# q times k as two 64-row by 120-column matmuls, scores packed without a gap, and one q tile loaded earlier

## The chip, the cores and the metric

The kernel runs on one core of one Trainium2 chip. The metric is the time of one execution in device microseconds, lower is better; the number quoted is the median of several runs. The profile is of one further execution.

## The reference, cut to what matters

Two parts follow each other: attention whose heads are mixed before and after the softmax ("talking heads"), then a bilinear feed-forward. Batch 4, 12 heads, 448 tokens, 64 channels a head; all in float32.

```python
scores = scale * np.matmul(q, k.transpose(0, 1, 3, 2))        # q times k
scores = np.einsum('bhij,hg->bgij', scores, w_pre)            # heads mixed
scores = scores - np.max(scores, axis=-1, keepdims=True)
attn = np.exp(scores)
attn = attn / (np.sum(attn, axis=-1, keepdims=True) + 1e-09)
attn = np.einsum('bhij,hg->bgij', attn, w_post)               # heads mixed again
x = np.matmul(attn, v)                                        # then [tokens, 768]
out = (x @ w_a * (x @ w_b)) @ w_out
```

## The kernel before

**Tiling of the attention.** Each batch's 448 query tokens are cut into chunks of 120, 120, 120 and 88. For each chunk, `qk(c, i)` makes the raw scores of two heads (i and i + 6) over all 448 keys. The channels of the two heads lie on SBUF rows 0 to 63 and 64 to 127, so `qk_head` is called with `g` = 0 and 1. For each head it issues two matmuls, one for each half of the chunk's tokens: a weight tile of 64 rows by 64 (or fewer) columns and a moving tile of 64 rows by 448. The first half goes to PSUM partitions 0 on, the second to partitions 64 on, so that for a chunk of 120 tokens the 4 partitions between hold nothing that is used. One `qk` is thus 4 matmuls, one in each quarter of the array; each float32 matmul stands in the trace as two records, each with a weight load of its own. One copy on VectorE or ScalarE (L304, L306) then moves both heads from PSUM (the one buffer of tag `t`) to the score tile `st[c]`.

**The order of tokens.** `spread_q` copies a loaded q tile (`qraw`, three heads of the chunk) into an order in which the five tokens of a half-block lie `nb` rows apart; `cut(n)` is where the second half begins (60 for n = 120).

**Units and steps.** A unit is 20 tokens of a chunk; there are 92 units, and the main loop runs one step `s` for each. `gather(u)` brings a unit's scores, by four SBUF-to-SBUF DMAs of 60 rows, into tiles `sb` in which heads and tokens share the partitions. `premix` (PSUM tile `mp`, L343) multiplies them with the mixing weights, `smax` takes maximum and exponential, `norm` prepares the second mixing matrix, `postmix` (`pp`, L389) applies it, `evac_p` copies it to `pt`, and `av` (`xp`, L427) multiplies with v. A step holds the premix of its unit, usually one `qk` for the next chunk, one `av` piece of the last group, and the postmix of the unit before. `premix`, `postmix` and `qk` are matmuls of 60 or 64 weight rows by 64 columns; `av` uses 128 rows by 64 columns; the matmuls of the feed-forward and of its first part (L637 to L639) 128 by 128.

**Start.** Before the loop, loads of q, k and the first 8 of 14 pieces of v (`V_EARLY`, L208 to L216) are issued on SyncE's queue (SP), in the order of the text. Up to unit 4, `gather` issues two of its four DMAs on SP and two on GpSimd's queue (POOL); later ones are all on POOL. POOL also runs `spread_q`. The `qraw` tiles have 3 buffers, so the fifth q tile waits for the copy of the second to be done.

**After step 90.** Feed-forward matmuls; the change does not touch them.

Of the kernel before, what the change touches and what calls it, by code (L numbers as in the profile page):

```python
# [22 lines left out]
def talking_heads_bilinear_kernel(  # L23
# [11 lines left out]
    nc = tc.nc  # L35
# [3 lines left out]
    QH = 5  # L39
    QB = 2 * QH  # L40
    QU = 2 * QB
    CHUNK = CHUNK_Q
    QG = 3
# [39 lines left out]
    chunks = []  # L83
    for b in range(B):
        t0 = 0
        while t0 < S:
            n = min(CHUNK, S - t0)
# [89 lines left out]
    def setup_w():  # L177
        nc.vector.memset(wp, 0.0)
        pre = wp[:, :QH * H].rearrange("p (i g) -> p i g", i=QH)
        shape = [64, QH, H]  # L180
        for e in range(2):
            rows = slice(64 * e, 64 * e + 64)
            nc.vector.tensor_tensor(
                pre[rows],
                wrep[rows, 0].unsqueeze(1).to_broadcast(shape),
                mask[rows, QH * e:QH * e + QH].unsqueeze(2).to_broadcast(shape),
                op=ALU.mult,
            )
        nc.vector.tensor_scalar(wp, wp, scale, None, op0=ALU.mult)
        nc.vector.tensor_tensor(tmask, mask[:, :QH], mask[:, QH:], op=ALU.add)  # L190
        shape = [128, H, QH]
        nc.vector.tensor_tensor(
            kf,
            wrep[:, 1].unsqueeze(2).to_broadcast(shape),
            tmask.unsqueeze(1).to_broadcast(shape),
            op=ALU.mult,
        )


    kt, kraw, qraw, qt = {}, {}, {}, {}  # L200
    st, sbt, mt, at, rss, krs, ptt, xps = {}, {}, {}, {}, {}, {}, {}, {}

    def load_v(b, i):
        g, i = divmod(i, V_PIECES // 2)
        to, of = vt[b % 2][g], v[b, g]
        if i < 3:
            heads = slice(2 * i, 2 * i + 2)
            nc.sync.dma_start(out=to[:C, heads], in_=of[:C, heads])  # L208
        elif i < 5:
            heads = slice(3 * (i - 3), 3 * (i - 3) + 3)  # L210
            nc.sync.dma_start(out=to[C:P, heads, :R - 1], in_=of[C:, heads, :R - 1])
        elif i == 5:
            for j in range(R - 1):
                nc.sync.dma_start(out=to[P:, :, j], in_=of[C + Y * j:C + Y * j + Y, :, R - 1])
        else:
            nc.sync.dma_start(out=to[C:, :, R - 1], in_=of[:C, :, R - 1])  # L216
# [4 lines left out]
    def part(half):  # L221
        return slice(0, 128) if half is None else slice(64 * half, 64 * half + 64)

    def load_k(b, i, half=None):
        if not half:
            if b == 0:
                if i == 0:
                    kraw["t"] = big.tile([128, G, S], F32, tag="pt", name="kraw")
                kraw[b, i] = kraw["t"][:, i]
            else:  # L230
                kraw[b, i] = k_p.tile([128, S], F32, tag="kraw", name="kraw", bufs=2)
        rows = part(half)
        nc.sync.dma_start(out=kraw[b, i][rows], in_=k[b, rows, i])

    def order_k(b, i, one=nc.vector.tensor_copy, two=nc.vector.tensor_copy):
        raw = kraw.pop((b, i)).rearrange("p (r x) -> p r x", r=R)
        kt[b, i] = k_p.tile([128, S], F32, tag="k", name="k")
        lo = kt[b, i][:, :R * C].rearrange("p (r x) -> p r x", r=R)
        hi = kt[b, i][:, R * C:].rearrange("p (r x) -> p r x", r=R - 1)
        one(lo, raw[:, :, :C])  # L240
        two(hi[:, :, :X], raw[:, :R - 1, C:])
        two(hi[:, :, X:], raw[:, R - 1, C:].rearrange("p (j l) -> p j l", j=R - 1))

    def load_q(c, j, half=None):
        b, t0, n = chunks[c]
        if not half:
            qraw[c, j] = q_p.tile([128, QG, CHUNK], F32, tag="qraw", name="qraw", bufs=3)[:, :, :n]
        rows, sl = part(half), slice(G * t0 + QG * j * n, G * t0 + QG * (j + 1) * n)
        nc.sync.dma_start(out=qraw[c, j][rows], in_=q[b, rows, sl].rearrange("d (h t) -> d h t", h=QG))

    def cut(n):
        nb, rest = divmod(n, QB)
        return QH * nb + min(rest, QH)

    def spread_q(c, j, eng=nc.gpsimd):
        n = chunks[c][2]
        nb = n // QB
        m, h0 = nb * QB, cut(n)
        t = q_p.tile([128, QG, CHUNK], F32, tag="q", name="q")[:, :, :n]
        raw = qraw.pop((c, j))  # L260
        for e in range(2):
            eng.tensor_copy(
                t[:, :, e * h0:e * h0 + QH * nb].rearrange("d h (i k) -> d h i k", k=nb),
                raw[:, :, :m].rearrange("d h (k i) -> d h i k", k=nb)[:, :, e * QH:(e + 1) * QH],
            )
        if m < n:
            r0 = h0 - QH * nb
            eng.tensor_copy(t[:, :, QH * nb:h0], raw[:, :, m:m + r0])
            if n - m > r0:
                eng.tensor_copy(t[:, :, h0 + QH * nb:], raw[:, :, m + r0:])  # L270
        qt[c, j] = t

    def qk_head(c, i, g, out):
        b, t0, n = chunks[c]
        rows = slice(D * g, D * g + D)
        h0 = cut(n)
        for e in range(2):
            cols = slice(0, 64) if e == 0 else slice(h0, n)
            nc.tensor.matmul(  # L279
                out[64 * e:64 * e + cols.stop - cols.start],  # L280
                lhsT=qt[c, i // QG][rows, i % QG, cols],
                rhs=kt[b, i][rows],
            )

    def qk(c, i, own=1):
        b, t0, n = chunks[c]
        m = 64 + n - cut(n)
        if c not in st:
            st[c] = (k_p if c % 3 == 2 else big).tile([128, H, S], F32, tag="s", name="s", bufs=1 if c % 3 == 2 else 2)
        if c <= 1 and i % 2 and i < QK_EARLY + 2 * (1 - c):  # L290
            for g in range(2):
                if i == 3:
                    sp = pp_t[g].rearrange("p x j t -> p (x j t)")[:, :S]
                else:
                    sp = ps.tile([128, 512], F32, tag="m", name="psq", bufs=3)[:, :S]
                qk_head(c, i, g, sp)
                nc.vector.tensor_copy(st[c][:m, g * G + i], sp[:m])
            return
        sp = ps.tile([128, 2, 512], F32, tag="t", name="pst", bufs=1)[:, :, :S]
        for g in range(2):  # L300
            qk_head(c, i, g, sp[:, g])
        to = st[c].rearrange("p (g i) s -> p i g s", g=2)[:m, i]
        if own:
            nc.vector.tensor_copy(to, sp[:m])  # L304
        else:
            nc.scalar.copy(to, sp[:m])  # L306

    def halves(n):
        return [(o, min(QH, n - o)) for o in range(0, n, QH)]

    def gather(u):
        c, o, n = units[u]
        sbt[u] = [sb_p.tile([128, S], F32, tag=f"sb{e}", name="sb") for e in range(2)]
        for i, (t, m) in enumerate(halves(n)):
            r = 64 * (i // 2)
            nb = chunks[c][2] // QB
            k_ = (o + t) // QB
            r0 = 64 * (t % QB // QH)
            if k_ < nb:
                rows = st[c][r0:r0 + QH * nb].rearrange("(i k) h s -> k i h s", k=nb)[k_]  # L320
            else:
                rows = st[c][r0 + QH * nb:r0 + QH * nb + m]
            (nc.sync if u <= AH and i % 2 else nc.gpsimd).dma_start(out=sbt[u][i % 2][r:r + m * H], in_=rows)  # L323
# [119 lines left out]
    for c in range(1, NC):  # L443
        b, t0, _ = chunks[c]
# [11 lines left out]
    for a in range(NA):  # L456
        b, u0, n = groups[a]
# [392 lines left out]
    with tc.manual_schedule():  # L850
# [16 lines left out]
        for i in range(G):  # L867
            if i == 1:
                spread_q(0, 1, nc.vector)
                setup_w()  # L870
            if i + 4 < G:
                load_k(0, i + 4)
                order_k(0, i + 4, pool, pool)
            if i == 2:
                load_q(1, 0)
                load_q(1, 1)
                for j in range(V_EARLY):
                    load_v(0, j)
            qk(0, i, 0)
# [2 lines left out]
        nxt_g = AH + 1  # L882
        for u in range(nxt_g):
            gather(u)
            if u == 2:
                load_q(2, 0)
                spread_q(2, 0)
            if u == 3:
                load_q(2, 1)
        for i in range(QK_EARLY):  # L890
            qk(1, i, 0)
        for r in range(2):
# [4 lines left out]
        for s in range(NU + 2):  # L897
# [3 lines left out]
            while nxt_g <= min(s + AH, NU - 1) and ready.get(units[nxt_g][0], -1) < s:  # L901
                gather(nxt_g)
                nxt_g += 1
# [110 lines left out]
        for n in range(NP * 2):  # L1014
            i, r = divmod(n, R6)
# [59 lines left out]
```

## Time and profile before

| | |
|---|---|
| three runs | 870.14, 873.02, 879.17 us; median 873.02 us |
| the profiled execution | 869.91 us, its span 868.2 us |
| PE busy | 839.9 us (97%) |
| PEld (weight loads) busy | 675.3 us (78%) |
| DVE, ACT, POOL busy | 500.0, 414.7, 476.3 us |
| L279 (q times k) | 728 records, 93.2 us busy |
| L343 (premix) | 720 records, 96.0 us busy |
| L389 (postmix) | 5040 records, 99.4 us busy |
| L427 (attention times v) | 1536 records, 93.3 us busy |

PE is the matmul part of TensorE, PEld its weight loads, DVE VectorE, ACT ScalarE, POOL GpSimd and SP SyncE. SPq is SP's queue of DMA issues. Matmul ends are modelled, so start times say more than durations: the difference between the starts of two groups of records is what the first group holds the engine for. Matmuls of different tiles of the array overlap, so busy times of two groups may overlap too.

### The profile page before, as it was taken

How to read it: one execution, taken by the hardware profiler on the slowest of the kernel's cores; microseconds unless marked ns; L12 is line 12 of the kernel's file. 1: busy time of each engine (PE TensorE's matmuls, PEld its weight loads, DVE VectorE, ACT ScalarE, POOL GpSimd, SP SyncE). 2: the span in 40 equal slices, each digit the busy share in tenths (PEclk: the TensorE clock that was granted, in tenths of full speed). 3: DMA queues.
4: the chain of work that ended last, by engine and by line, in shares of the span. 5: the costliest groups of instructions: out<-in, count | busy, mean ns of one | idle time of the engine just before them, and what ended most of it. 6: DMA issues, size and time to landing. Idle time of an engine off the chain costs nothing.

```text
span 868.2 us, 26219 instructions
## 1 busy us (share of the span) xinstructions
PE 839.9 (97%) x10612; PEld 675.3 (78%) x10612; DVE 500.0 (58%) x989; ACT 414.7 (48%) x864; POOL 476.3 (55%) x591
## 2 busy tenths in 40 slices
PE   8899999999999899999999999999999999999998
PEld 4455665656556565798999999999999998999997
DVE  5577677868787777355533433354445345655762
ACT  3576676767767688544323322332233145333330
POOL 5775686767757876026447433668666743222220
PEclk9999999999999999999999999999999999999999
DMA  7797799788867986673644643656665497564551
GB/s 188 183 194 174 164 219 192 180 183 200 203 161 180 209 218 137 182 242 134 199 133 162 191 152 132 217 192 237 221 233 183 146 327 291 199 232 182 203 204 66
DMA packets 105730, 165.90 MB, mean 191 GB/s; under 512 B 50278, under 2 KB 81618, under 8 KB 105610
## 3 DMA queue, kind: packets, MB, share of 16 engines
q1 hardware_dynamic: 77482, 126.54, 46.6%
q0 software_dynamic: 28128, 37.68, 19.2%
q8 instruction: 84, 1.38, 0.7%
q14 instruction: 36, 0.29, 0.1%
HBM read 84.16 MB, written 41.29 MB: 144 GB/s over the span
## 4 chain that ended last, share of the span: by engine, by line
PE 78%; DMA 9%; POOL 4%; issue 3%; DVE 3%; SPq 1%; ACT 1%; DVEq 0%; POOLq 0%
PE xp L427 6%; PE pp L389 6%; PE pb L639 6%; PE pa L637 6%; PE pa L638 6%; PE pa L639 6%; PE pb L638 6%; PE pb L637 6%; PE po L757 6%; PE po L758 6%; PE pst L279 6%; PE po L756 6%; PE mp L343 5%; DMA sb<-s 4%; POOL sb L323 3%
## 5 line engine op out<-in xcount | busy, mean ns | idle before, releaser
L323 POOL DMA_DIRECT2D sb<-s x350 | 201.9, 591 | 55.5 <-PE mp L343 19.5
L356 ACT ACTIVATE a<-mp,nm 124x448 f32<-124x448 f32 x180 | 112.7, 631 | 63.2 <-DVE nm L353 63.2
L353 DVE TENSOR_REDUCE nm<-mp 124x1 f32<-124x448 f32 x180 | 104.0, 618 | 55.1 <-PE mp L343 54.3
L659 DVE TENSOR_TENSOR hf<-pb,sa 128x448 f32<-128x448 f32 x47 | 29.3, 624 | 169.2 <-PE pb L639 153.7
L427 PEld LDWEIGHTS xp<-pt,v 128*64 128x64 f32 x1536 | 73.8, 136 | 61.9 <-issue 43.5
L643 ACT COPY sa<-pa 128x448 f32<-128x448 f32 x47 | 25.2, 536 | 174.6 <-PE pa L639 174.6
L406 ACT COPY pt<-pp 128x480 f32<-128x480 f32 x176 | 91.2, 575 | 33.9 <-PE pp L389 33.4
L389 PE MATMUL pp<-kr,a 60*64 60x60 f32 x5040 | 99.4, 222 | 7.6 <-issue 7.1
L389 PEld LDWEIGHTS pp<-kr,a 60*64 60x64 f32 x5040 | 86.6, 135 | 24.9 <-issue 13.7
L639 PE MATMUL pb<-xhl,wl 128*128 128x448 f32 x282 | 102.3, 363 | 0.9 <-POOL wl L622 0.9
L637 PE MATMUL pb<-xhl,wh 128*128 128x448 f32 x282 | 102.2, 362 | 0.0
L638 PE MATMUL pb<-xhl,wh 128*128 128x448 f32 x282 | 102.2, 362 | 0.0
L279 PE MATMUL pst<-k,q 64*64 64x448 f32 (+1 forms) x728 | 93.2, 549 | 8.0 <-DVE s L304 4.8
L343 PE MATMUL mp<-sb,wp 60*64 60x448 f32 x720 | 96.0, 550 | 3.6 <-DMA sb<-s 3.0
L637 PE MATMUL pa<-xhl,wh 128*128 128x448 f32 x264 | 95.7, 362 | 0.0
L638 PE MATMUL pa<-xhl,wh 128*128 128x448 f32 x264 | 95.7, 362 | 0.0
L639 PE MATMUL pa<-xhl,wl 128*128 128x448 f32 x264 | 95.7, 362 | 0.0
L427 PE MATMUL xp<-pt,v 128*64 128x120 f32 (+1 forms) x1536 | 93.3, 265 | 0.8 <-ACT pt L406 0.8
L628 POOL TENSOR_TENSOR wl<-v,wh 128x768 fp32r<-128x768 f32 x21 | 39.2, 1867 | 98.9 <-ACT wh L627 96.4
L757 PE MATMUL po<-hhl,wh 128*128 128x448 f32 x252 | 91.6, 363 | 1.6 <-DVE hhl L715 1.6
L758 PE MATMUL po<-hhl,wl 128*128 128x448 f32 x252 | 91.4, 363 | 0.0
L756 PE MATMUL po<-hhl,wh 128*128 128x448 f32 x252 | 91.3, 362 | 0.0
(117 smaller groups left out, 1432.3 us busy)
## 6 DMA issues: line engine op xcount, KB each, us to landing
sb<-s POOLq DMA_DIRECT2D x346, 105.0 KB, 5.2
hhl<-hd SPq DMA_DIRECT2D x42, 448.0 KB
v<-in_w_ab_dram SPq DMA_DIRECT2D x22, 768.0 KB
hd<-hf SPq DMA_DIRECT2D x48, 224.0 KB
v<-in_w_out_dram SPq DMA_DIRECT2D x12, 768.0 KB
wod<-cw SPq DMA_DIRECT2D x21, 384.0 KB
v<-wod SPq DMA_DIRECT2D x21, 384.0 KB
xhl<-xd SPq DMA_DIRECT2D x24, 224.0 KB
```

Of the source, the lines that this page charges most:

```text
L279: nc.tensor.matmul(out[64 * e:64 * e + cols.stop - cols.start], lhsT=qt[c, i // QG][rows, i % QG, cols], rhs=kt[b, i][rows],)
L323: (nc.sync if u <= AH and i % 2 else nc.gpsimd).dma_start(out=sbt[u][i % 2][r:r + m * H], in_=rows)
L343: nc.tensor.matmul(mt[u, i // 2][col:col + M], lhsT=wp[r:r + m, :M], rhs=tiles[i % 2][r:r + m])
L356: nc.scalar.activation(a[:m], mp[:m], ACTF.Exp, bias=nm[:m], scale=1.0, accum_out=rss[u][:m, j:j + 1])
L389: nc.tensor.matmul(pp_t[i][C * e:C * e + C, H * r:H * r + H, j, :m], lhsT=at[u, j][rows, x:x + C], rhs=kr[rows, j, :, :m],)
L427: nc.tensor.matmul(xp[64 * e:64 * e + 64, p % 3, :n], lhsT=vt[b % 2][g][:, h % G, r], rhs=ptt[a][:, r, h, :n], start=(r == 0), stop=(r == ...
L637: nc.tensor.matmul(o, lhsT=hh[:, off + k], rhs=x[:, 0, k], start=first, stop=False)
L638: nc.tensor.matmul(o, lhsT=hh[:, off + k], rhs=x[:, 1, k], start=False, stop=False)
L639: nc.tensor.matmul(o, lhsT=ll[:, off + k], rhs=x[:, 0, k], start=False, stop=last)
L756: nc.tensor.matmul(po, lhsT=hh[:, k], rhs=t[:, 0, k], start=(k == 0), stop=False)
L757: nc.tensor.matmul(po, lhsT=hh[:, k], rhs=t[:, 1, k], start=False, stop=False)
L758: nc.tensor.matmul(po, lhsT=ll[:, k], rhs=t[:, 0, k], start=False, stop=(k == KH2 - 1))
```

## The change

`qk_head` issues one matmul for each head, with a weight tile of 64 rows by all n tokens of the chunk (120 or 88 columns), which writes PSUM partitions 0 to n - 1. The score rows have no gap any more: copies move n rows (`m`) and `gather` finds the second half at row `cut(n)`. In the start, the load of the third chunk's first q tile, `load_q(2, 0)`, stands ahead of the early loads of v, where it stood behind the gathers of units 0 to 2, and its `spread_q` stands behind all five first gathers, where it stood behind the third.

```diff
     def qk_head(c, i, g, out):
         b, t0, n = chunks[c]
         rows = slice(D * g, D * g + D)
-        h0 = cut(n)
-        for e in range(2):
-            cols = slice(0, 64) if e == 0 else slice(h0, n)
-            nc.tensor.matmul(
-                out[64 * e:64 * e + cols.stop - cols.start],
-                lhsT=qt[c, i // QG][rows, i % QG, cols],
-                rhs=kt[b, i][rows],
-            )
+        nc.tensor.matmul(out[:n], lhsT=qt[c, i // QG][rows, i % QG], rhs=kt[b, i][rows])
 
     def qk(c, i, own=1):
         b, t0, n = chunks[c]
-        m = 64 + n - cut(n)
+        m = n
...
-            r0 = 64 * (t % QB // QH)
+            r0 = cut(chunks[c][2]) * (t % QB // QH)
...
             if i == 2:
                 load_q(1, 0)
                 load_q(1, 1)
+                load_q(2, 0)
                 for j in range(V_EARLY):
                     load_v(0, j)
             qk(0, i, 0)
...
         for u in range(nxt_g):
             gather(u)
-            if u == 2:
-                load_q(2, 0)
-                spread_q(2, 0)
             if u == 3:
                 load_q(2, 1)
+        spread_q(2, 0)
         for i in range(QK_EARLY):
             qk(1, i, 0)
```

## Rows read from the trace of the kernel before

**Rows 1.** Page, chain that ended last: share of the span by engine.
```profile
PE 78%; DMA 9%; POOL 4%; issue 3%; DVE 3%; SPq 1%; ACT 1%; DVEq 0%; POOLq 0%
```

**Rows 2.** Windows: stretch, its length, busy us (records) by engine, PEclk, DMA share, GB/s.
```profile
53.00:77.00 24.00, 21.68 (x528) 12.59 (x520) 17.41 (x49) 15.45 (x39) 15.77 (x28) 1.00 0.93 194
...
77.00:230.00 153.00, 148.57 (x3724) 92.45 (x3723) 112.67 (x278) 109.55 (x269) 108.37 (x203) 1.00 0.83 188
230.00:262.00 32.00, 29.24 (x737) 17.03 (x733) 27.08 (x72) 22.17 (x55) 17.86 (x32) 1.00 0.77 173
262.00:292.00 30.00, 30.00 (x742) 18.31 (x732) 22.01 (x54) 22.06 (x54) 24.81 (x44) 1.00 0.83 194
...
304.00:327.00 23.00, 23.00 (x560) 14.02 (x552) 17.93 (x42) 19.23 (x46) 16.85 (x31) 1.00 0.90 217
```

**Rows 3.** Windows of line 279 (q times k) alone: PE and PEld busy (records).
```profile
77.00:230.00 153.00, 42.60 (x344) 14.04 (x344) 1.00 0.83 188
230.00:262.00 32.00, 7.70 (x64) 1.95 (x64) 1.00 0.77 173
262.00:292.00 30.00, 9.21 (x72) 2.88 (x72) 1.00 0.83 194
...
304.00:327.00 23.00, 6.62 (x56) 2.10 (x56) 1.00 0.90 217
```

**Rows 4.** Timeline of PE, one step from 151.55 us: start, length, line, tiles, records.
```profile
151.55 0.94 PE L343 MATMUL mp<-sb,wp 60*64 60x448 f32 x8
152.31 0.93 PE L279 MATMUL pst<-k,q 64*64 64x448 f32 x8
153.17 1.04 PE L427 MATMUL xp<-pt,v 128*64 128x120 f32 x16
154.15 1.04 PE L389 MATMUL pp<-kr,a 60*64 60x60 f32 x56
155.01 0.56 PE L343 MATMUL mp<-sb,wp 60*64 60x448 f32 x4
```

**Rows 5.** Timeline of PE: from 128 weight columns to 64, rows unchanged.
```profile
366.86 0.37 PE L638 MATMUL pst<-xhl,wh 128*128 128x448 f32 x1
367.06 0.36 PE L639 MATMUL pst<-xhl,wl 128*128 128x448 f32 x1
367.35 0.75 PE L427 MATMUL xp<-pt,v 128*64 128x88 f32 x14
```

**Rows 6.** Timeline of PE: the first 128-column matmuls behind postmix.
```profile
348.34 0.47 PE L637 MATMUL pst<-xhl,wa 128*128 128x448 f32 x1
348.65 0.37 PE L638 MATMUL pst<-xhl,wa 128*128 128x448 f32 x1
```

**Rows 7.** Timeline of SP's queue in the start: DMA issues by line.
```profile
6.19 2.22 SPq L208 DMA_DIRECT2D v<-in_v_dram  x3
...
12.86 0.62 SPq L208 DMA_DIRECT2D v<-in_v_dram  x1
14.58 6.76 SPq L323 DMA_DIRECT2D sb<-s  x6
21.39 1.03 SPq L249 DMA_DIRECT2D qraw<-in_q_dram  x1
```

**Rows 8.** Timeline of DVE: the copy of the second q tile.
```profile
8.99 0.72 DVE L262 COPY q<-qraw 128x180 f32<-128x180 f32 x2
```

**Rows 9.** Timeline of POOL: third chunk's q tile, then gathers of units 3 on.
```profile
26.11 0.93 POOL L262 COPY q<-qraw 128x180 f32<-128x180 f32 x2 [7.42 <-DMA qraw<-in_q_dram]
26.98 4.59 POOL L323 DMA_DIRECT2D sb<-s  x8
```

**Rows 10.** Timeline of PE: premix of unit 0 and of unit 3, idle before.
```profile
18.86 1.55 PE L343 MATMUL mp<-sb,wp 60*64 60x448 f32 x5 [0.79 <-DMA sb<-s]
...
31.14 1.52 PE L343 MATMUL mp<-sb,wp 60*64 60x448 f32 x5 [2.25 <-DMA sb<-s]
```

**Rows 11.** Windows: the granted clock behind that wait (seventh figure).
```profile
32.00:34.00 2.00, 2.00 (x19) 1.49 (x14) 0.57 (x2) 0.00 (x0) 1.47 (x3) 0.50 0.87 191
```

## The prediction

> **What bounds the kernel now.** I read the chain that ended last first. By engine it is 78% TensorE [rows 1], so an edit on PE counts, if it falls in a stretch where PE sets the pace. The change touches only the attention, and so the windows over that part come next. Between 77 and 230 us PE is busy 148.6 of 153 us, between 262 and 292 and between 304 and 327 us without a gap [rows 2]. Between 230 and 262 us it idles 2.8 us, and in 53 to 77 us 2.3 us with the DMA engines 93% busy [rows 2]: there something else decides now and then. Then the timeline of one step shows what a step consists of: premix, q times k, attention times v, postmix, and after 3.46 us (155.01 - 151.55) the next premix, with nothing idle between [rows 4]. In such steps a longer q times k lengthens the step by as much. The number of them: the records of line 279 are 8 to a `qk`, so 344, 72 and 56 records are 43, 9 and 7 steps [rows 3], together 59; another 8 lie between 230 and 262 us.
>
> The second thing to read is the start. Premix of unit 3 waits 2.25 us for its gather [rows 10]; that gather was issued on POOL at 26.98 us, behind a copy which had waited 7.42 us for the third chunk's q tile [rows 9]; and that tile was issued on SP only at 21.39 us, behind six gathers [rows 7]. Behind the gap the granted clock is at 0.50, that is at 1.2 instead of 2.4 GHz, for a whole window of 2 us [rows 11].
>
> **The body of q times k.** Now four matmuls of 64 by 64 fill the four quarters of the array; afterwards two of 64 by 120 fill its two halves. Premix, four quarters too, holds the engine 0.76 us (152.31 - 151.55) for two passes [rows 4], so one pass of 448 columns takes 0.38 us with all quarters at work. Two halves that work at once need the same two passes: 0.76 us. Halving the number of matmuls and weight loads thus saves nothing here, since the passes set the time. Copies of 120 instead of 124 rows take as long, because they go by columns. The gathers read as many rows as before. Both at nothing.
>
> **What the wider weights cost.** From premix to q times k nothing about the tile changes today, and the 0.76 us are bare. From q times k to attention times v (64 by 64 to 128 by 64) it is 0.86 us for the same two passes (153.17 - 152.31) [rows 4]: 0.10 us are lost at the change of tile. Is it the rows or the columns that cost? One place in the trace changes columns alone: from 128 by 128 to 128 by 64 it takes 0.29 us where the steady spacing is 0.20 us (367.35 - 367.06 against 367.06 - 366.86) [rows 5], so 0.09 us are lost with the rows unchanged. After the change premix (64 by 64) to q times k (64 by 120) is such a change of columns, in every step, and q times k to attention times v remains one: one more per step, 0.10 us. The Trainium skill (TensorEngine Tiling (Array Packing), Key Properties) says that changing the tiling mode, not just the tile, drains the TensorE; the trace agrees, with the 0.09 and 0.10 us just read, and by that rule the change costs time.
>
> The second cost lies behind such a change. The first 128-column matmul behind postmix holds the engine 0.31 us (348.65 - 348.34) [rows 6] against 0.20 us steady [rows 5]: its weights are not there yet, 0.11 us. For 120 columns I take 120/128 of it, 0.10 us, once, as the loads of the two row halves can run side by side. Sum for each `qk`: 0.10 + 0.10 = 0.20 us. Bounds: 0.09 us if the weights still come ahead of time, 0.31 us if two loads follow each other (0.10 + 2 x 0.105).
>
> Over the 59 steps: 59 x 0.20 = 11.8 us. The others I cost at nothing: between 230 and 262 us and before 77 us, waits for loads and copies cover 0.2 us a step (PE idles 2.8 us in some nine steps, 2.3 us in some six) [rows 2]; without that cover it is 14 x 0.2 = 2.8 us more. In the first steps a `qk` is followed by a copy out of its single PSUM buffer, and PE waits for it.
>
> **The moved load.** `load_q(2, 0)` takes the buffer of the second q tile, whose copy on DVE is done at 8.99 + 0.72 = 9.71 us [rows 8]. SP reaches the load before 6.19 us, where v starts today [rows 7], and stands there until 9.71 us. Queued behind it are the eight pieces of v (10 DMAs), and behind these SP's half of the gathers. With 0.6 us for the load itself, as a piece of v takes [rows 7], v starts at about 10.3 us, 4.1 us late, and ends at 13.48 + 4.1 = 17.6 us; the gathers of units 0 to 2, which start at 14.58 us today [rows 7], start at 17.6 us. So units 0 to 2 are 3.0 us late, and PE's 0.79 us before premix 0 [rows 10] becomes 3.8 us.
>
> On the other side POOL no longer waits: its gathers of units 3 and 4 go out at 26.11 - 7.42 = 18.69 us, eight microseconds earlier [rows 9]. Unit 3 now waits for SP's half: 17.6 + 6.76 us for the six before it = 24.4 us, 2.25 us for its own two (a third of 6.76) [rows 7], then 2.0 us to land (premix 0 starts at 18.86 us [rows 10], and the first two of the six are out at 14.58 + 2.25 = 16.8 us): about 28.6 us instead of 31.14 us, a gain of 2.5 us. The slow clock I leave out of the sum: the long gap before premix 0 is likely to bring it there instead. Bounds: a loss of 3 us if the delay of units 0 to 2 is never made up; a gain of 5.5 us if v costs SP nothing, so that its two gathers of unit 3 follow the six as early as the q load does today (21.39 + 2.25 + 2.0 = 25.6 us). What follows up to 77 us runs with DMA engines 93% busy [rows 2]; as all of it is paced by the steps, I let the gain through.
>
> **Sum.** 11.8 - 2.5 = 9.3 us. On the profiled execution, 869.9 us with its span of 868.2, that gives 879.2 us; it lies 3.1 us below the median of the runs, so that on the median, 873.0 us, the forecast is **882 us**, about 1.1% slower.
>
> **Rivals.** (a) The weights still arrive during premix, and only the change of tile costs: 59 x 0.10 - 2.5 = 3.4 us, 876 us. For it: weight loads do run ahead within one tile shape. Against: the 0.31 us [rows 6].
> (b) Width alone costs nothing in this place, since both row halves stay: then only the start is left, -2.5 us, 870.5 us, at best 867.5 us: not slower. It decides if premix to q times k stays at 0.76 us. Against: the 0.29 us with unchanged rows [rows 5].
> (c) The gap in SP's queue is not made up by unit 3, and the start loses its 3 us: 873 + 11.8 + 3 = 888 us. For it: v ends 4 us later in my own sum.
> (d) Two tiles of 64 rows by 128 columns do not run at once: 0.76 us more in each of the 59 + 8 `qk`, 51 us, with the rest 933 us or more. Against: premix does run both row halves at once [rows 4]; but in 64-column tiles, and no row shows 64 by 128.
>
> **How the numbers follow.** Forecast 0.45; (a) 0.17; (b) 0.13; (c) 0.18; (d) 0.07. A measurement of this kernel tells about 1%, 8.7 us, from no change. The forecast's own range is 877 to 889 us: 0.15 to 0.25 us a step with a start between -5 and 0 us. The whole range, 869 to 893 us, takes in (a), (c), most of (b), and leaves (d) out; its upper end is 59 steps at 0.31 us, 18.3 us, with a start at +1.7. Slower by over 1% (above 881.7 us): about 0.6 of the forecast, most of (c), all of (d), 0.51. Within 1%: the rest of the forecast, (a) and most of (b), 0.42. Faster by over 1% (below 864.3 us) needs more than (b)'s best start: 0.07.
>
> **What would show it.** A step between 77 and 230 us should last 3.66 us instead of 3.46; premix to q times k 0.86 instead of 0.76 us, q times k to attention times v 0.96 instead of 0.86 us. If the former stays at 0.76 us, (b) holds; if the latter stays at 0.86, (a); if it is above 1.5 us, (d). In the start, v should begin near 10 us on SP, POOL's 7.4 us wait be gone, premix 0 come near 22 us and premix of unit 3 near 28.6 us; if the latter comes behind 31 us, (c) holds. The feed-forward behind 370 us should take as long as before; if it does not, something is at work that I have not seen.

## The result, and the profile after

The changed kernel is slower by 0.6%: 878.22 us median against 872.28 us, ratio 1.0057 with a 95% interval of 1.0036 to 1.0079, or 5.0 us (3.1 to 6.9). The forecast was 882 us with a range of 869 to 893. The profiled execution has a span of 878.8 us, against 868.2: these two executions lie 10.6 us apart, twice the measured difference, so what is read from them stage by stage adds up to too much.

Line numbers are 7 lower from `qk_head` on: L276 is the q-times-k matmul (before L279), L336 premix, L382 postmix, L420 attention times v, L316 the gathers, L346 the maximum.

The page's chain that ended last, by engine, has TensorE at 86% now, where it had 78% [rows 1]:

```profile
PE 86%; DMA 3%; DVE 3%; POOL 2%; issue 2%; SPq 1%; ACT 1%; DVEq 0%; POOLq 0%
```

The timeline of PE over one step of a 120-token chunk (start, length, line, tiles, records), to be held against [rows 4]:

```profile
92.93 0.94 PE L336 MATMUL mp<-sb,wp 60*64 60x448 f32 x8
93.80 1.02 PE L276 MATMUL pst<-k,q 64*120 64x448 f32 x4
94.74 1.04 PE L420 MATMUL xp<-pt,v 128*64 128x120 f32 x16
95.71 1.04 PE L382 MATMUL pp<-kr,a 60*64 60x60 f32 x56
96.57 0.94 PE L336 MATMUL mp<-sb,wp 60*64 60x448 f32 x8
```

Premix to q times k takes 0.87 us (it was 0.76), q times k to attention times v 0.94 us (0.86), the step 3.64 us (3.46). That is 0.11 us at the change of tile and 0.08 us for weights that are not there yet, 0.19 us together. The timeline of PEld shows the latter: in the kernel before, weight loads of q times k begin 0.37 us ahead of its first matmul at 152.31 us [rows 4], in the changed kernel with it, at 93.79 us (first before, then after):

```profile
151.94 0.15 PEld L279 LDWEIGHTS pst<-k,q 64*64 64x64 f32 x4 [0.22 <-issue]
...
93.79 0.29 PEld L276 LDWEIGHTS pst<-k,q 64*120 64x120 f32 x4 [0.70 <-ACT pt L399]
```

For a chunk of 88 tokens the second figure shrinks with the columns:

```profile
152.81 0.94 PE L336 MATMUL mp<-sb,wp 60*64 60x448 f32 x8
153.68 0.99 PE L276 MATMUL pst<-k,q 64*88 64x448 f32 x4
154.59 1.04 PE L420 MATMUL xp<-pt,v 128*64 128x120 f32 x16
```

Here q times k holds the engine 0.91 us instead of 0.94. The two row halves do run at once: four records in the time of eight.

The start looks quite unlike what was forecast. SP's queue, as in [rows 7]:

```profile
4.57 5.79 SPq L249 DMA_DIRECT2D qraw<-in_q_dram  x3
10.41 1.83 SPq L208 DMA_DIRECT2D v<-in_v_dram  x3
...
16.03 1.61 SPq L208 DMA_DIRECT2D v<-in_v_dram  x1
17.76 11.48 SPq L316 DMA_DIRECT2D sb<-s  x8
```

The third of the three q loads waits for its buffer; v begins at 10.41 us instead of 6.19, and the gathers at 17.76 instead of 14.58. Then eight gathers take 11.48 us to go out, 1.4 us each; before, six took 6.76 us. POOL, as in [rows 9]:

```profile
15.49 5.77 POOL L316 DMA_DIRECT2D sb<-s  x10 [2.65 <-DVE s L290]
21.17 1.02 POOL L262 COPY q<-qraw 128x180 f32<-128x180 f32 x2
```

POOL does not wait for the q tile any more, and its ten gathers of units 0 to 4 go out in one run. But the first unit's data from SP's queue take 7.38 us to land, by the chain of waits,

```profile
17.76 7.38 DMA sb<-s
```

and PE, whose premix of unit 0 stands in [rows 10] at 18.86 us, does half of it at 19.50 us and the other half at 25.18 us:

```profile
19.50 1.45 PE L336 MATMUL mp<-sb,wp 60*64 60x448 f32 x4 [1.24 <-DMA sb<-s]
25.18 2.89 PE L336 MATMUL mp<-sb,wp 60*64 60x448 f32 x4 [4.23 <-DMA sb<-s]
```

In this gap the granted clock falls, and it is 0.50 from 24 to 32 us (windows; the seventh figure is the clock), where [rows 11] have that for one window of 2 us:

```profile
24.00:28.00 4.00, 2.82 (x5) 0.57 (x5) 0.62 (x1) 0.37 (x1) 0.00 (x0) 0.50 0.49 140
28.00:32.00 4.00, 4.00 (x15) 1.25 (x16) 2.59 (x6) 1.08 (x4) 1.73 (x3) 0.50 0.59 177
```

How far the units have come is read from the start of their first maximum on DVE, which follows premix. Against the kernel before, the changed one is 6.3 us late at unit 0, 8.8 at unit 2, 4.2 at unit 4, 2.1 at unit 13 and 9.0 at the last unit; behind the attention another 1.6 us come in these two executions. In them the start thus lost 2 us where it was to gain 2.5, and the steps from 13 on lost 7 where they were to lose 12.

The 1.6 us stand in the feed-forward, which was to take as long as before, and the granted clock shows them. Both kernels have a wait of PE for DVE of 1.28 us there; behind it the clock falls in the changed kernel (first line) and not in the kernel before (second line):

```profile
730.00:733.00 3.00, 3.00 (x11) 2.66 (x11) 1.16 (x2) 1.19 (x4) 0.00 (x0) 0.61 1.03 415
...
721.00:724.00 3.00, 3.00 (x16) 2.81 (x16) 1.16 (x2) 1.21 (x4) 0.00 (x0) 1.00 1.02 415
```

The experiment with the load behind v, further below, has the same fall behind the same wait (its clock is 0.50 from 727 to 729 us), the other experiments that move the start do not: it is not tied to the wide weights, and from one profile of each kernel no run tells how often it comes.

### The profile page after: what moved, and what is told of

Read it like the earlier page. It is cut to its first block, busy times and chain, and to the rows that moved or that the text cites. A ratio compares the mean times of both kernels' runs of the same rounds, so it can differ in the third digit from the quotient of the medians.

```text
span 878.8 us, 25451 instructions
## 1 busy us (share of the span) xinstructions
PE 854.2 (97%) x10228; PEld 671.6 (76%) x10228; DVE 501.9 (57%) x989; ACT 415.2 (47%) x864; POOL 476.2 (54%) x591
## 3 DMA queue, kind: packets, MB, share of 16 engines
q0 software_dynamic: 28128, 37.68, 17.6%
## 4 chain that ended last, share of the span: by engine, by line
PE 86%; DMA 3%; DVE 3%; POOL 2%; issue 2%; SPq 1%; ACT 1%; DVEq 0%; POOLq 0%
PE xp L420 9%; PE pp L382 8%; PE pst L276 8%; PE mp L336 7%; PE pb L632 6%; PE pa L630 6%; PE pa L631 6%; PE pa L632 6%; PE pb L631 6%; PE pb L630 6%; PE po L750 6%; PE po L751 6%; PE po L749 6%; POOL sb L316 1%; DMA sb<-s 1%
## 5 line engine op out<-in xcount | busy, mean ns | idle before, releaser
L316 POOL DMA_DIRECT2D sb<-s x350 | 201.6, 589 | 68.3 <-PE mp L336 36.2
L346 DVE TENSOR_REDUCE nm<-mp 124x1 f32<-124x448 f32 x180 | 104.1, 619 | 66.5 <-PE mp L336 66.1
L420 PEld LDWEIGHTS xp<-pt,v 128*64 128x64 f32 x1536 | 73.9, 136 | 58.8 <-issue 38.1
L382 PE MATMUL pp<-kr,a 60*64 60x60 f32 x5040 | 97.8, 222 | 6.3 <-issue 5.7
L382 PEld LDWEIGHTS pp<-kr,a 60*64 60x64 f32 x5040 | 84.4, 134 | 24.7 <-issue 16.9
L336 PE MATMUL mp<-sb,wp 60*64 60x448 f32 x720 | 93.9, 549 | 5.6 <-DMA sb<-s 5.5
L276 PE MATMUL pst<-k,q 64*120 64x448 f32 (+1 forms) x364 | 93.2, 588 | 3.4 <-DVE s L297 1.9
L420 PE MATMUL xp<-pt,v 128*64 128x120 f32 (+1 forms) x1536 | 93.4, 265 | 1.1 <-ACT pt L399 0.8
```

The lines of the kernel that those rows point to most:

```text
L276: nc.tensor.matmul(out[:n], lhsT=qt[c, i // QG][rows, i % QG], rhs=kt[b, i][rows])
L336: nc.tensor.matmul(mt[u, i // 2][col:col + M], lhsT=wp[r:r + m, :M], rhs=tiles[i % 2][r:r + m])
L382: nc.tensor.matmul(pp_t[i][C * e:C * e + C, H * r:H * r + H, j, :m], lhsT=at[u, j][rows, x:x + C], rhs=kr[rows, j, :, :m],)
L420: nc.tensor.matmul(xp[64 * e:64 * e + 64, p % 3, :n], lhsT=vt[b % 2][g][:, h % G, r], rhs=ptt[a][:, r, h, :n], start=(r == 0), stop=(r == ...
```

## The experiments

Each runs against the kernel before. Its ratio carries a 95% interval; 0.1% is 0.87 us.

### The unchanged kernel, timed like an experiment

> The kernel before, unchanged, timed like an experiment: how far apart two programs that are the same come out. Theory: ratio 1.000, within 0.3%. Rival (the comparison puts every experiment some 0.3% above, as the four runs that moved loads, copies or gathers, 1.0026 to 1.0039, make one suspect): 1.003.

Measured: 0.9985 (0.9955 to 1.0015). In this series nothing is added by the comparison itself, and differences below 0.3% are not told from nothing. In its profile units 1 and 2 come 1.0 and 1.2 us later than in the first profile of the same kernel, and unit 13 comes 1.1 us earlier; shifts of that size between two profiles say nothing.

### Only the wide weights

The hunks of `qk_head`, `qk` and `gather`'s row are kept, the moved load and copy are put back.

> Only the wide weights of the change; loads and copies of the start stand as in the kernel before. Theory (tile price): the two traces show premix to q times k at 0.868 us instead of 0.757 and q times k to attention times v at 0.946 instead of 0.863, 0.19 us for each qk; from step 13 to the end of the attention the changed kernel fell 7.0 us further behind (2.06 us to 9.03 us). With the start untouched this kernel should be slower than the one before by about 5 to 8 us, ratio 1.006 to 1.009, and unit 3's premix should come at the 31 us of before. Rival (the start is the whole loss): within 2 us of the kernel before.

Measured: 1.0043 (1.0013 to 1.0073), 3.7 us (1.1 to 6.3). The wide weights alone make the kernel slower; its steps show the same 0.87 and 0.94 us. Of the rival (within 2 us) only the lower end of the interval is left, 1.1 to 2 us. The size is below what was expected, and unit 3's maximum came 2.0 us later than before in this profile, unit 13's 2.4 us, not at the same time: the changed kernel's 2 us at unit 13 need not be all due to the moved load.

### Only the moved load and copy

Column halves stay.

```diff
                 load_q(1, 1)
+                load_q(2, 0)
                 for j in range(V_EARLY):
...
-            if u == 2:
-                load_q(2, 0)
-                spread_q(2, 0)
...
+        spread_q(2, 0)
```

> Only the moved load and copy; q times k in column halves as before. Theory (start loses): SP waits with the load for the second q tile's copy, v and the first gathers come late, and unit 2's maximum should come 7 to 9 us later than the 26.0 us of before; the transfers behind it are paced by the steps and find freer DMA engines, so that at 77 us 0 to 3 us are left: ratio 1.000 to 1.004. Rival (the start gains, as predicted): 2.5 us faster, ratio 0.997.

Measured: 1.0032 (0.9996 to 1.0067). The maxima of units 0 to 4 come at 27.21, 31.00, 33.66, 37.28 and 41.32 us, where the kernel before has 20.72, 23.38, 26.04, 33.43 and 37.95 us:

```profile
27.21 1.32 DVE L353 TENSOR_REDUCE nm<-mp 124x1 f32<-124x448 f32 x2 [8.61 <-PE mp L343]
31.00 1.15 DVE L353 TENSOR_REDUCE nm<-mp 124x1 f32<-124x448 f32 x2
33.66 1.15 DVE L353 TENSOR_REDUCE nm<-mp 124x1 f32<-124x448 f32 x2
```

Unit 2 is 7.6 us late, unit 4 3.4 us and unit 13 3.1 us. The rival (a gain of 2.5 us) falls: 0.9971 lies below the interval. With the wide weights' 0.43% the two parts make 0.75%, which the measured 0.57% does not contradict.

### The load behind v instead of ahead of it

```diff
                 for j in range(V_EARLY):
                     load_v(0, j)
+                load_q(2, 0)
...
-            if u == 2:
-                load_q(2, 0)
-                spread_q(2, 0)
...
+        spread_q(2, 0)
```

> Column halves as before; the load of the third chunk's first q tile directly behind the early pieces of v instead of ahead of them, its copy behind all five first gathers. Theory (SP's order is what costs in the start, POOL's wait is what could be saved): SP reaches the load at 13.5 us, when its buffer has been free since 9.7 us, so nothing waits; units 0 to 2 come as before, unit 3's premix at 26 to 29 us instead of 31.1 us, and 2 to 4 us of this remain at 77 us: ratio 0.995 to 0.998. Rival (the loads between 40 and 77 us set the pace whatever the start does): the gain is gone by 77 us, ratio 1.000.

Measured: 1.0026 (0.9995 to 1.0058). The theory falls. The rival's ratio of 1.000 lies in the interval, but there is no early gain to lose: SP waits for no buffer here and the last piece of v goes out only 0.8 us later than before, yet unit 1 is 5.6 us late and unit 2 8.4 us. The chain of waits names a gather that SP issued at 19.6 us and that took 9.54 us to land:

```profile
19.64 9.54 DMA sb<-s
```

So the held queue of SP cannot be the whole cause. What this run shares with the change and with the load moved alone is that POOL waits for no q tile: nine gathers go out there in one run from 15.30 us, and the tenth at 21.08 us.

### Only the copy moved

```diff
             if u == 2:
                 load_q(2, 0)
-                spread_q(2, 0)
             if u == 3:
                 load_q(2, 1)
+        spread_q(2, 0)
```

> One thing moved against the kernel before: the POOL copy of the third chunk's first q tile stands behind the gathers of units 3 and 4; its load stays behind the gathers of units 0 to 2 on SP, column halves stay. Theory (POOL's 7.4 us wait held POOL's gathers of units 3 and 4 back while SP's halves of units 1 and 2 landed): POOL's gathers go out at 18.7 us, SP's halves land late, as in the run with the load behind v (9.5 us for one), and unit 2's maximum comes 4 to 9 us later than at 26.0 us. Rival (SP's own order makes units 0 to 2 late): units 0 to 2 as before, unit 3's premix at 26 to 29 us instead of 31.1 us, some 3 us gained. Time, by the theory: 0 to 3 us slower, ratio 1.000 to 1.004.

Measured: 1.0039 (1.0002 to 1.0076). SP's order is that of the kernel before (its gathers begin at 15.60 us, 1.0 us later); only POOL is free of its wait. POOL's ten gathers go out from 15.36 us, by POOL's timeline in this kernel:

```profile
15.36 5.77 POOL L323 DMA_DIRECT2D sb<-s  x10 [1.07 <-DVE s L297]
```

A gather that SP issued at 18.25 us takes 8.22 us to land, by its chain of waits:

```profile
18.25 8.22 DMA sb<-s
```

The maxima of units 1, 2 and 3 follow, by the timeline of DVE:

```profile
25.67 0.62 DVE L353 TENSOR_REDUCE nm<-mp 124x1 f32<-124x448 f32 x1
...
31.39 1.16 DVE L353 TENSOR_REDUCE nm<-mp 124x1 f32<-124x448 f32 x2 [0.16 <-PE mp L343]
34.03 1.15 DVE L353 TENSOR_REDUCE nm<-mp 124x1 f32<-124x448 f32 x2
```

Unit 1 is 2.3 us late, unit 2 5.4, and unit 3 comes 0.6 us later than before: POOL's half of its gathers went out eight microseconds earlier, but SP's half at 25.17 us, 2.7 us later than before (22.46). The theory holds for the order of events: POOL's wait is what kept the transfers of units 3 and 4 out of the way of those of units 1 and 2. For the time it says less: at unit 13 this profile is level with the kernel before, at the last unit 1.8 us ahead, and the ratio just clears 1. Its span is 8.6 us longer all the same, and all of that comes in the feed-forward, which the edit leaves alone: from 420 to 700 us PE starts 1402 matmuls in the kernel before (first line) and 1356 here, both at full clock.

```profile
420.00:700.00 280.00, 280.00 (x1402) 262.85 (x1401) 115.02 (x123) 79.97 (x113) 167.27 (x101) 1.00 0.56 188
...
420.00:700.00 280.00, 280.00 (x1356) 253.37 (x1355) 112.98 (x122) 78.39 (x110) 161.32 (x96) 1.00 0.52 177
```

No other profile has that in this stretch, and no run shows why; what the copy alone costs stays open.

### Units 3 and 4 gathered behind the others on one queue

```diff
-            (nc.sync if u <= AH and i % 2 else nc.gpsimd).dma_start(...)
+            (nc.sync if u <= AH and (i % 2 or u > 2) else nc.gpsimd).dma_start(...)
```

with the load behind v and the copy behind the gathers.

> Column halves; load of the third chunk's first q tile behind v, its copy behind the first gathers, and all four gathers of units 3 and 4 on SP's queue, behind those of units 0 to 2 (before: two on SP, two on POOL). Theory (two queues with the gathers of different units side by side delay the more urgent ones): with SP's queue in order of need units 0 to 2 come within 1.5 us of before (20.7, 23.4, 26.0 us), unit 3's premix at 26 to 30 us instead of 31.1 us, and 0 to 3 us of that are left at 77 us: ratio 0.997 to 1.000. Rival (any earlier gather of units 3 and 4 costs the first units as much as it gains): units 1 and 2 come over 3 us late here too, ratio 1.000 to 1.004.

Measured: 1.0034 (1.0003 to 1.0064). Units 0 to 2 come within 1.3 us of before, so order protects them; unit 3 is 0.7 us earlier, unit 4 0.6 us later. SP needs 10.86 us for ten gathers:

```profile
15.00 10.86 SPq L323 DMA_DIRECT2D sb<-s  x10
```

The theory holds for who is late, but nothing is gained by it, and its ratio (0.997 to 1.000) fails. Unit 4's maximum comes at 37.95 us in the kernel before, at 38.28 us with the copy alone moved and at 38.52 us here; at 41.32 us with the load alone moved, 41.36 us with the load behind v, 42.14 us in the change, and at 41.42 us with the wide weights alone, although that kernel starts in the order of the one before. The granted clock divides these kernels in the same way. From 20 to 42 us its mean is 0.92 in the three with the earlier unit 4, 0.84 in three of the later ones and 0.77 in the change (first the kernel before, then the wide weights alone):

```profile
20.00:42.00 22.00, 17.99 (x326) 9.76 (x320) 12.51 (x29) 11.76 (x29) 14.78 (x30) 0.92 0.70 179
...
20.00:42.00 22.00, 18.54 (x230) 7.38 (x230) 10.76 (x25) 9.88 (x24) 13.57 (x27) 0.84 0.60 172
```

In the second profile of the unchanged kernel it is 1.00, and unit 4 comes at 36.86 us. A clock lower by 0.08 over 22 us takes 1.8 us of PE's time, over half of what lies between the two groups. The order decides which unit waits; whether the clock brings unit 4 to the later time, or units that are late anyway leave PE idle and so bring the clock down, no run settles.

### More changes of tile, without any wide weights

Each step's attention times v is cut in two, one half ahead of q times k and one behind: the same matmuls, four changes of tile shape in a step instead of two. The hunk that lets `av` take half of its rows is left out here.

```diff
-            for it in items.get(s, ()):
+            its = list(items.get(s, ()))
+            if len(its) == 2 and its[0][0] is qk and its[1][0] is av:
+                its = [(av, *its[1][1:], (0, 1)), its[0], (av, *its[1][1:], (2, 3))]
+            for it in its:
```

> The kernel before, with the attention-times-v matmuls of a step cut into two halves, one ahead of q times k and one behind it: the same matmuls in another order, with four changes of tile shape in a step instead of two. Theory (each change has a price, 0.10 us for the change and 0.05 us for weights of 64 columns that no longer come ahead): 2 x 0.155 = 0.31 us more for each step, a step of 3.76 us where it is 3.45 us, and with 60 to 100% of 59 steps 11 to 18 us: ratio 1.013 to 1.021. Rival (the price belongs to the wide weights alone): ratio 1.000.

Measured: 1.0108 (1.0068 to 1.0149), 9.4 us, below the range that was expected, though its lower end (1.013) lies in the interval. A step is 3.75 us in the timeline, 0.3 us more:

```profile
150.30 1.04 PE L389 MATMUL pp<-kr,a 60*64 60x60 f32 x56
151.16 0.94 PE L343 MATMUL mp<-sb,wp 60*64 60x448 f32 x8
152.03 0.63 PE L427 MATMUL xp<-pt,v 128*64 128x120 f32 x8
152.59 0.98 PE L279 MATMUL pst<-k,q 64*64 64x448 f32 x8
153.49 0.63 PE L427 MATMUL xp<-pt,v 128*64 128x120 f32 x8
154.05 0.34 PE L389 MATMUL pp<-kr,a 60*64 60x60 f32 x8
```

The price belongs to the change of tile and not to wide weights: premix to attention times v takes 0.87 us here, q times k in halves 0.90 us. It also shows the missing part again: 69 steps (units 13 to 81) of 0.3 us are 21 us, and 9 are seen.

### Fewer changes of tile

The six pieces of a group stand in four steps (`AV_AT = (1, 1, 3, 4, 4, 6)`), or three by three in two (`(2, 2, 2, 5, 5, 5)`).

> Column halves; the six attention-times-v pieces of a group stand in four steps (two, one, two, one) instead of six, so that a pair has one entry and one exit of the 128 by 64 tile in place of two. Theory (each change of tile shape costs 0.155 us with its weights): 2 x 0.31 us less in six steps, over 69 steps 7.1 us of PE work less; as the waits of the attention take up over half of such a difference (split_av: 18 us of work added, 9 us seen), 2 to 5 us faster, ratio 0.994 to 0.998. Rival (steps without such a piece are too short for the other engines, PE waits): 1.000 or slower.

Measured: 0.9981 (0.9951 to 1.0012), not told from no change; most of the theory's range and the rival's 1.000 both lie in the interval, so neither falls.

> Column halves; the six pieces of a group stand three by three in two steps. Theory: 4 x 0.31 us less in six steps, over 69 steps 14 us of PE work less, of which 4 to 8 us are seen, ratio 0.991 to 0.996. Rival (a step without a piece has 2.4 us of PE work against some 2.5 us each on DVE and ACT and 2.3 us on POOL, a step with three 5.1 us; with buffers for one step the engines wait in turn): slower, ratio 1.00 to 1.02.

Measured: 1.0044 (1.0014 to 1.0074), slower; the rival holds. In its attention (76 to 336 us) PE idles 17.5 us; with column halves and a piece in each step it is about 10. Of this it waits 5.5 us in 13 places for ScalarE's copy of the score buffer before it can start a q times k, by the list of waits (what, total us, times, longest):

```profile
PE pst L279 <- ACT s L306: 5.5, 13, 0.7
```

No version was found that beats the kernel before by more than the measurement tells.

### Where the rest of the price goes

The stretch from unit 13 to unit 82 lasts 251.1 us in the kernel before. With column halves and the main loop unchanged there are six profiles of it (the kernel before twice, and the four that touch the start): 249.1 to 256.0 us, mean 252.7. With wide weights it is 254.4 (alone) and 258.0 us (the change), mean 256.2; with the split 261.6 us. So 3.5 us are seen of 69 x 0.19 = 13.1 us, and 8.9 of 21. The windows of that stretch, rounded to whole microseconds (stretch, length, busy time of PE, its weight loads and the other engines, clock, DMA share, GB/s), first of the kernel before:

```profile
74.00:326.00 252.00, 242.37 (x6032) 148.95 (x6024) 189.55 (x465) 181.08 (x439) 178.61 (x328) 0.99 0.83 190
```

The same window of the wide weights alone:

```profile
76.00:331.00 255.00, 250.57 (x5748) 145.23 (x5748) 189.95 (x466) 180.96 (x439) 178.57 (x329) 1.00 0.80 188
```

Of the change:

```profile
76.00:334.00 258.00, 251.09 (x5748) 145.49 (x5744) 189.47 (x465) 180.96 (x438) 179.31 (x330) 1.00 0.77 186
```

And of the split:

```profile
73.00:335.00 262.00, 257.65 (x6026) 140.00 (x6026) 190.22 (x465) 182.54 (x439) 180.56 (x330) 1.00 0.76 183
```

PE idles 9.6 us before (7.9 to 12.1 in the six profiles, mean 9.8), 4.4 and 6.9 us with wide weights, 4.4 us with the split: with more work on PE, 3 to 5 us of its waits are gone. In the kernel before, the largest entry in the list of waits is postmix waiting for nothing that the profile names ("issue"; what, total us, times, longest). This entry in four kernels, in this order: the kernel before, the wide weights alone, the change, the split.

```profile
PE pp L389 <- issue: 7.1, 7, 2.4
...
PE pp L382 <- issue: 2.4, 4, 1.4
...
PE pp L382 <- issue: 5.7, 6, 2.5
...
PE pp L389 <- issue: 1.0, 2, 0.7
```

The six profiles with column halves have 3.4 to 9.1 us of it, 3.7 us in the second of the unchanged kernel, and the change lies among them: that it is this wait that shrinks is not shown. What these waits are for no run settles.

A part lies in the clock. The kernel before has some half clock in a stretch of the attention in which PE idles 2.4 us:

```profile
292.00:304.00 12.00, 9.56 (x239) 6.11 (x241) 7.89 (x17) 6.99 (x18) 9.88 (x20) 0.86 1.00 210
```

That is 12 x 0.14 = 1.7 us of PE's time. Three of the six profiles (the load moved, the load behind v, units 3 and 4 on one queue) have twice as much, the other two none, 2.0 us in the mean. With wide weights and with the split there is none between units 13 and 82. Of the 9.6 us that wide weights do not show, less idle time thus makes 4.1 us and the clock up to 2.0; the remaining 3.5 us lie in time that counts as busy, and stay open.

By steps the picture is plainer. The median of the 69 steps, from one unit's maximum to the next, is 3.45 us in each of the six profiles, 3.65 us in both with wide weights and 3.76 us with the split: a typical step shows the whole price. But 20 to 28 of the 69 steps last over 3.5 us with column halves. If the steps are parted at 3.5 us by the mean of three of the six profiles, and the split is held against the other three, the shorter half of the steps carries 7.7 of its 8.9 us and the longer half 1.2 (means over all ways to take three).

## Why the prediction was right, and where its steps were not

**The sign and the time** were right: 5 us slower, where 9.3 were forecast, and 878 us lie in the narrower range (877 to 889) too. It lies within 1%, a case given 0.42, where slower by more had 0.51; the interval does keep it clear of no change. But two of the sum's terms missed, with opposite signs: the weights by 8 of 11.8 us, by the run that has them alone, and the start by 5.3 us, twice its own size. That the total came within the range is to that extent luck. (By its own terms, 59 x 0.25 us with a start at 0, the narrower range ends at 888 us.)

**The body of q times k** was right: nothing was saved by half as many matmuls, and rival (d) is out, as four records of 64 by 120 take the time of eight.

**The price of a `qk`** was right: 0.20 us forecast, 0.11 + 0.08 = 0.19 us measured, and in the two places named. Rivals (a), where the weights would have come ahead of time, and (b), where the width would have cost nothing, fall by the 0.94 and 0.87 us. By the Trainium skill (TensorEngine Tiling (Array Packing), Key Properties), a changed tiling mode drains the TensorE; the runs agree, as far as lost time goes, for a change of columns alone (0.11 us) and, with the split, for one of rows alone (0.11 us from premix to attention times v).

**The number of steps that show it** was the term that was mis-sized. "PE without a gap" was read off windows in which PE is busy nearly all the time, and 59 steps were counted in full, 11.8 us. Only steps that last as long as their parts, 3.45 us as a rule, show it in full; the windows hide steps of 4 to 5 us among them. Wide weights alone measured 3.7 us (1.1 to 6.3), start included, and the profiles 3.5 of 13 us; the split, 9.4 of 21. That part of the cover lies in waits inside the stretches called bound is shown by the idle time and by the split's longer steps; what PE waits for in the largest part of them stays open.

**The moved load** was wrong: the run that has it alone excludes the forecast gain of 2.5 us, and all but shows a loss. That SP would wait until 9.7 us, that v would start at 10.3 us and the gathers near 17.6 us came true: the third q load was out at 10.36 us (4.57 + 5.79), v began at 10.41 and the gathers at 17.76 us. The step that failed is "then some 2.0 us to land", with six gathers in 6.76 us. The 2.0 us were misread: premix 0 at 18.86 us begins, by the kernel's text, with what POOL's gathers bring, and its start says nothing of SP's. In the kernel before, SP's fourth gather goes out at 17.21 us (first line, of the chain that ended last), and the premix of unit 1 waits for it until 22.61 us (second line, of the timeline), 5.4 us from issue:

```profile
17.21 0.74 SPq L323
...
22.61 0.19 PEld L343 LDWEIGHTS mp<-sb,wp 60*64 60x64 f32 x2 [0.26 <-DMA sb<-s]
```

That was with six gathers of POOL's beside SP's; with ten, those of SP's that set the pace took 7.4 to 9.5 us to land, and SP needed some 1.4 us for each to go out. The prediction counted what POOL's vanished wait would release as a gain and did not ask what it would collide with; moving the copy alone made unit 2 5.4 us late. Units 0 to 2 were 6.3 to 8.8 us late, not 3.0, and unit 3 came at no gain. Rival (c) came nearest, a start that loses 3 us: the load and copy alone measured 2.8 us (-0.3 to 5.8), and its own condition held, unit 3 behind 31 us. It missed the total for the same over-counted steps.

**That a delay passes on** was only partly right. Of 8.8 us at unit 2, 4.5 are left at unit 3 in the changed kernel, 4.2 at unit 4 and 2.1 at unit 13; with the load alone it is 3.1 of 7.6 at unit 13. The first half is made up before 38 us, since the kernel before has its own wait ahead of unit 3 [rows 10]. Between 53 and 77 us the DMA engines are 77% busy now, where they were 93% [rows 2], and PE 23.77 of 24 us:

```profile
53.00:77.00 24.00, 23.77 (x526) 13.41 (x520) 19.02 (x53) 16.52 (x40) 17.63 (x32) 1.00 0.77 204
```

Part of the other half is taken up there. That the steps of the start pace the loads is the likely reason; no run separates it. The long gap did bring the slow clock to premix 0, as the prediction says, but for longer than it had been at unit 3: the mean from 20 to 42 us is 0.77 against 0.92, and 22 x 0.15 = 3.3 us of PE's time for which the sum had no term.

## What to carry to other kernels

Fewer and wider matmuls save nothing if the passes already fill the array, and cost something in every place where the new tile shape stands between others: count the changes of shape in a loop, not the instructions. An engine that is 97% busy can still hide half of a small price; multiply it by the steps whose length is exactly the sum of their parts, not by all steps of a busy stretch. Before a stall is removed, ask which transfers it was holding back and whose they will meet. Take a transfer's time to land from the instruction that needs that very transfer.

## What the runs showed of the hardware

A change of tile shape on TensorE costs 0.09 to 0.11 us between float32 matmuls, also when only the columns change, and then the weights: 0.04 to 0.05 us more for 64 and 88 columns, 0.08 us for 120, 0.11 us for 128. SBUF-to-SBUF gathers of 105 KB on SP's queue land 4.2 to 5.7 us after their issue where PE waits for them in the two profiles of the kernel before, with six of POOL's beside them; they take 7.4 to 9.5 us when POOL has ten in flight, while the windows show the DMA engines at some 50 to 90%. It need not be POOL's queue that is full: with units 3 and 4 on SP's, a gather that SP issued at 24.24 us is waited for until 31.69 us. A gap at the start can leave TensorE at half clock for longer than the gap: 0.50 from 24 to 32 us in the change, with 4.2 us of waiting and with PE at work all through the second half of that. And behind the same wait of 1.28 us in the feed-forward the clock fell in the change, to 0.61 in the mean from 730 to 733 us, and stayed at 1.00 in the kernel before.
